# Where three engines' code lies: a second fetch block entered at the start, and 44 sums as a loop

## The chip, the core and the metric

The kernel runs on one core of a Trainium2 chip. A core has engines that each run their own instruction stream: TensorE (PE, matrix products), VectorE (DVE), ScalarE (ACT), GpSimd (POOL) and SyncE (SP, which here issues the loads). 16 DMA engines move data between device memory and the core. The metric is the device time of one execution in microseconds, lower is better.

## What is computed

One decoding step of a transformer block, batch 2, one new token, width 448, 16 heads of 256, a cache of 8192 keys and values for each head and batch entry, all in float32:

```python
q = (layernorm(x) @ wq)                                   # per head, per batch entry
scores = einsum("bhqd,bhkd->bhqk", q, k_cache) * Dh**-0.5
p = softmax(scores)
h = x + (einsum("bhqk,bhkd->bhqd", p, v_cache)) @ wo
n = layernorm(h)
out = h + ((n @ w_gate) * (n @ w_up)) @ w_down
```

Keys and values are 16 x 2 x 8192 x 256 floats each, 8 MB for every pair of head and batch entry, 537 MB in all. Each is used once.

## The kernel before

There are 32 pairs of head and batch entry (`NQ`). For each, 8192 keys lie as 128 partitions x 64 rows x 256. VectorE multiplies them with the query, which stands on every partition (`keys_times`, L358), and sums over the 256 (`summed`, L363); it takes the highest score (`highest`, L366). TensorE turns that column (`top`), VectorE negates its maximum (`negated`, L369), TensorE spreads it (`bias`), ScalarE takes the exponentials (`softmax`, L375), and TensorE multiplies them with the values (`mix`, L336: 32 products of two rows each). `turned` (L345) and L559 bring the result through `wo`, and `query` (L272, L277) makes the next head's query.

Pairs 1 to 30 run in hardware loops (`nc.Fori`), one for each of VectorE, ScalarE and TensorE, of 15 rounds with two pairs each; they meet through semaphores that are counted up by one engine and taken by another (`tell_of`, `take`, L319). SyncE's loads are written out in order: keys of a pair, values of the pair before, every eight pairs a piece of the weights. Keys have room for nearly two pairs, values for one, so each load waits until the last user of its room is done.

Ahead of the loops x is loaded (L185, by ScalarE's queue), turned by four transposes on TensorE (L241), and normalised in short steps between VectorE and TensorE (L244 to L266); then TensorE makes the queries of four heads (L272 to L302). [...] Its loop has 221 instructions, its whole program 1266, VectorE's 113, ScalarE's 161.

Behind the loops comes the last pair, then the two layers of the second half. For the last pair VectorE multiplies the keys in four parts of 16 rows; ScalarE sums rows 0 to 43 (`BY_ACT = 44`), one activation with accumulation and one read of the accumulator for each, written out (L526 to L529), VectorE sums the other 20. SyncE waits for both (L573) before it issues the second and third part of the last values (`LAST = (32, 24, 8)` rows) and the gate weights (L581), then the up weights (L583), then w_down in four pieces (`DOWN = (7, 4, 2, 1)` tiles, L587). TensorE follows: the last `mix`, the output projection, the gate and up products (L719) and the products with w_down (L778), which wait for each piece. VectorE copies the result (L785) and SyncE stores it.

Of the kernel before, what the change touches and what calls it, by code (L numbers as in the profile page):

```python
# [4 lines left out]
AF = mybir.ActivationFunctionType  # L5
ALU = mybir.AluOpType
AX = mybir.AxisListType
PE, DVE, ACT = (getattr(mybir.EngineType, n) for n in ("PE", "DVE", "Activation"))

B, D, H, SK, DH, F = 2, 448, 16, 8192, 256, 1792  # L10
EPS = 1e-5
P = 128
HALF = 64
DC = 4
# [3 lines left out]
HC = 16  # L18
# [9 lines left out]
BY_ACT = 44  # L28
# [45 lines left out]
def decode_block(nc, x, k_cache, v_cache, w, wg, wu, wd, out):  # L74
# [4 lines left out]


    names = ("x", "w", "k0", "k1", "k0a", "v", "g", "p", "d", "a", "zero", "dp", "ap", "pd", "pa", "da")
    names += ("dd", "aa", "gp", "first", "mixed", "heads")
    S = {n: Sem(nc, n) for n in names}
    late = [Sem(nc, f"late{i}") for i in range(len(LAST) + 1 + 2 + len(DOWN))]
    done = Sem(nc, "out")
    pe, dve, act, sp, pool = (
        Engine(e) for e in (nc.tensor, nc.vector, nc.scalar, nc.sync, nc.gpsimd)
    )

    def p_(instr):  # L90
        return S["p"].by(instr)

    def v_(instr):
        return S["d"].by(instr)

    def a_(instr):
        return S["a"].by(instr)
# [4 lines left out]
    def place(name, shape, offset=None):  # L102
        size = 4
        for n in shape[1:]:
            size *= n
        if offset is None:
            offset = at[0]
            at[0] += -(-size // 32) * 32
        return nc.alloc_sbuf_tensor_at(name, list(shape), F32, offset=offset).ap()
# [9 lines left out]
    ident = place("ident", (P, P))  # L119
# [3 lines left out]
    s_t = [place(f"s{i}", (P, NJ)) for i in range(2)]  # L123
# [15 lines left out]
    x_sb = place("x_sb", (B, DC * P))  # L139
# [30 lines left out]
    xT_ps = banks[6][:, : DC * B].rearrange("p (c b) -> p c b", b=B)  # L170
# [9 lines left out]
    def k_at(i, lo=0, hi=NJ):  # L180
        first = i % 2 * (NJ - OVER)
        return kb[:, first + lo : first + hi, :]


    x_in = S["x"].by(nc.scalar.dma_start(x_sb[:, :D], x.rearrange("b s d -> (b s) d")), 16)  # L185
    w_in = {0: S["w"].by(nc.sync.dma_start(wb[:, WQ:], w[0][:, WQ:]), 16)}

    def load_k(i, lo=0, hi=NJ, sem=None):
# [6 lines left out]
    t = S["g"].by(nc.gpsimd.memset(ident, 0.0))  # L195
    pool.wait(t)
    g_id = S["g"].by(
        nc.gpsimd.affine_select(
            out=ident, in_=ident, compare_op=ALU.not_equal, fill=1.0, base=0,
            pattern=[[-1, P]], channel_multiplier=1,  # L200
        )
    )
# [6 lines left out]
    def over_chunks(got, t):  # L209
        tok = v_(  # L210
            nc.vector.tensor_reduce(
                got, t[:, : DC - 1].rearrange("p c b -> p b c"), axis=AX.X, op=ALU.add
            )
        )
        dve.wait(tok)
        return v_(
            nc.vector.scalar_tensor_tensor(
                got, t[:, DC - 1, :], 0.5, got, op0=ALU.mult, op1=ALU.add
            )
        )  # L220
# [15 lines left out]
    )  # L236
    dve.wait(x_in)
    t = v_(nc.vector.tensor_copy(x_sb[:, D:], x_sb[:, D - HALF : D]))
    pe.wait(g_id, x_in, t)
    for c in range(DC):  # L240
        got = nc.tensor.transpose(xT_ps[:, c, :], x_sb[:, c * P : (c + 1) * P], ident[:B, :B])  # L241
    t = p_(got)
    dve.wait(t)
    t = v_(nc.vector.tensor_copy(xT, xT_ps))  # L244
    dve.wait(t)
    t = over_chunks(sum_x, xT)
    pe.wait(v_ones, t)
    t = p_(nc.tensor.matmul(mean_ps, ones, sum_x, start=True, stop=True))
    dve.wait(t)
    t = v_(  # L250
        nc.vector.scalar_tensor_tensor(
            xc, mean_ps[:, None, :].to_broadcast([P, DC, B]), -1.0 / D, xT,
            op0=ALU.mult, op1=ALU.add,
        )
    )
    dve.wait(t, g_xb)
    x_spread = spread(xb, xc, P)
    t = v_(nc.vector.tensor_mul(sq, xc, xc))
    dve.wait(t)
    t = over_chunks(sum_sq, sq)  # L260
    pe.wait(t)
    t = p_(nc.tensor.matmul(var_ps, ones, sum_sq, start=True, stop=True))
    act.wait(t, v_eps)
    t = a_(nc.scalar.activation(std, var_ps, AF.Sqrt, bias=eps_t, scale=1.0 / D))
    dve.wait(t)
    t = v_(nc.vector.reciprocal(rstd, std))  # L266
# [51 lines left out]
    def take(e, sem, n=1):  # L318
        e.wait_ge(S[sem].h, n).then_inc(S[sem].h, -n)  # L319

    def tell_of(instr, sem):
        instr.then_inc(S[sem].h, 1)
# [30 lines left out]
    last_act = []  # L353
    last = NQ - 1
    queries = qb.rearrange("p h b d -> p (h b d)")

    def keys_times(kt, q, to=None):
        return nc.vector.tensor_mul(  # L358
            kt if to is None else to, kt, q[:, None, :].to_broadcast([P, kt.shape[1], DH])
        )  # L360

    def summed(i, lo, hi, kt):
        return nc.vector.tensor_reduce(s_t[i % 2][:, lo:hi], kt, axis=AX.X, op=ALU.add)  # L363
# [4 lines left out]
    def negated():  # L368
        return nc.vector.tensor_reduce(nm, mT_ps, axis=AX.X, op=ALU.max, negate=True)  # L369
# [46 lines left out]
    first = v_(summed(0, NJ - HC, NJ, vb[:, :HC, :]))  # L416
    take(nc.vector, "k0", 16)
    t = v_(keys_times(k_at(0, 0, NJ - HC), qb[:, 0, 0]))
    dve.wait(t)
    t = v_(summed(0, 0, NJ - HC, k_at(0, 0, NJ - HC)))  # L420
# [4 lines left out]
    with nc.Fori(0, H - 1, engines=[DVE]) as g:  # L425
        for n in (1, 2):
            b = n % B
            off = nc.vector.snap((g + n // 2) % HEADS * (B * DH))
            q = queries[:, bass.ds(off + b * DH, DH)]
            parts = ((0, HC), (HC, NJ)) if b else ((NJ - HC, NJ), (0, NJ - HC))  # L430
            kt = k_at(n, *parts[0])
# [8 lines left out]
            kt = k_at(n, *parts[1])  # L440
# [7 lines left out]
    t = v_(  # L448
        nc.vector.tensor_reduce(
            sel16, ident.rearrange("p (g b r) -> p b r g", b=B, r=R)[:, :, 0, :],  # L450
            axis=AX.X, op=ALU.add,
        )
    )
# [5 lines left out]
    t = v_(  # L459
        nc.vector.tensor_scalar(  # L460
            share, sel16[:, None, :].to_broadcast([P, DC + 1, B]), -1.0 / D, None, op0=ALU.mult
        )
    )
# [12 lines left out]
    q = qb[:, (H - 1) % HEADS, B - 1]  # L476
    take(nc.vector, "k1", 16)
    dve.wait(behind(last - 1, 0))
    told["nm", last - 1] = v_(negated())
    ready = [v_(keys_times(k_at(last, 0, HC), q))]  # L480
    dve.wait(behind(last - 1, 2))
    d_rl[last - 1] = v_(nc.vector.reciprocal(rl_t[0], l_ps))
    for lo in range(HC, NJ, HC):
        ready.append(v_(keys_times(k_at(last, lo, lo + HC), q)))
    dve.wait(ready[-1])
    summed_last = v_(summed(last, BY_ACT, NJ, k_at(last, BY_ACT, NJ)))


# [1 line left out]
    with nc.Fori(0, H - 1, engines=[ACT]) as g:  # L490
        for b in range(B):
# [9 lines left out]
            got = turned_out(b, 0)  # L501
        tell_of(got, "ap")
        off = nc.scalar.snap(g % HEADS * (B * DH))
        for b in range(B):
            take(nc.scalar, "pa")
            got = nc.scalar.activation(  # L506
                queries[:, bass.ds(off + b * DH, DH)], q_ps[b], AF.Copy, scale=rstd[:, b : b + 1]
            )
# [14 lines left out]
        told["oT", i] = a_(turned_out(k, k))  # L523

    ends(last - 1)
    for k in range(BY_ACT):  # L526
        act.wait(ready[k // HC])
        kt = k_at(last)[:, k, :]
        t = a_(nc.scalar.activation(kt, kt, AF.Copy, accum_out=s_t[1][:, k : k + 1]))  # L529
    last_act.append(t)  # L530
    summed_at[last] = summed_last
    dve.wait(last_act[0], summed_last)
    told["m", last] = v_(highest(last))
# [6 lines left out]
        nc.gpsimd.sem_inc(S["gp"].h, HEADS)  # L540


    with nc.Fori(0, H - 1, engines=[PE], head_slot={PE: 0}) as g:
        with nc.Fori(0, B, engines=[PE]):
            take(nc.tensor, "dp")
            tell_of(top(), "pd")
            take(nc.tensor, "dp")
            tell_of(bias(), "pa")
            take(nc.tensor, "ap")
            tell_of(whole(), "pd")  # L550
            take(nc.tensor, "v", 16)
            tell_of(mix(0, NJ, vb), "pa")
            take(nc.tensor, "ap")
            tell_of(turned(), "pa")
        take(nc.tensor, "ap")
        take(nc.tensor, "gp")
        off = nc.tensor.snap(g % HEADS * WH)
        for c in range(2):
            nc.tensor.matmul(  # L559
                acc_ps, oT.rearrange("p c b r -> p c (b r)")[:, c], wb[:, bass.ds(off + c * D, D)],  # L560
                start=False, stop=False,
            )
        for b in range(B):
            tell_of(query(off, b), "pa")
# [4 lines left out]
    v_parts, lo = [], 0  # L569
    for n in LAST:  # L570
# [3 lines left out]
        to = kb[:, lo : lo + n, :]  # L574
# [9 lines left out]
    wd_in, lo = {}, 0  # L584
# [61 lines left out]
    lo, hi, v, there = v_parts[-1]  # L646
# [24 lines left out]
    def group(w, q):  # L671
# [8 lines left out]
        start=True, stop=False,  # L680
    )
    dve.wait(t_hq)
    t = v_(nc.vector.tensor_mul(mean_h, share, total[:, None, :].to_broadcast([P, DC + 1, B])))  # L683
    pe.wait(t)
    t = p_(
        nc.tensor.matmul(
            xc_ps.rearrange("p c b -> p (c b)"), ones, mean_h.rearrange("p c b -> p (c b)"),
            start=False, stop=True,
        )
    )  # L690
# [9 lines left out]
    t = v_(nc.vector.tensor_copy(xc_h, xc_ps[:, :DC]))  # L700
    dve.wait(t)
    t = v_(nc.vector.tensor_mul(sq_h, xc_h, xc_h))
    dve.wait(t)
    t = over_chunks(sum_h, sq_h)
# [36 lines left out]
    t = v_(nc.vector.tensor_scalar_add(ve, varh_ps, EPS))  # L741
# [30 lines left out]
    for k in range(NF):  # L772
        n, g = FF[k]
# [3 lines left out]
        for q in range(YN):  # L777
            got = nc.tensor.matmul(  # L778
                y_ps[32 * q : 32 * q + 32, :],
                hmT[n // 2][:, n % 2, g].rearrange("p b r -> p (b r)"),  # L780
                wd_t[:, k, q * YW : (q + 1) * YW], start=False, stop=(k == NF - 1),
            )
    t = p_(got)
    dve.wait(t)
    t = v_(nc.vector.tensor_copy(y, y_ps))  # L785
# [10 lines left out]
    t = done.by(nc.sync.dma_start(rows, eight(y)), 16)  # L796
# [60 lines left out]
```

## Time and profile before

| | |
|---|---|
| median of 3 runs (lowest to highest) | 1303.93 us (1303.85 to 1303.99) |
| the profiled execution | 1303.78 us |
| its span, first to last instruction | 1302.5 us |
| busy share of the span | DVE 86%, PE 38%, ACT 7% |
| DMA | 561.31 MB, 431 GB/s read over the span |
| instruction packets | queue q8: 5, 0.08 MB; queue q14: 3, 0.02 MB |

The profile is of one execution. Times in its rows are microseconds from the start of the span; "L336" is a line of the kernel. A row of the DMA part gives packets, bytes, and the time that they took as a share of 16 engines over the stretch. "hardware_dynamic" is data, "instruction" is code. In a row of stretches a packet counts with its whole length where it starts, so a short stretch can show a share above 1.

### The profile page before, as it was taken

Reading aid. Unit: us, or ns where it says so; the run is one execution under the profiler, and the core shown is the slowest. Engines: PE = TensorE matmul, PEld = TensorE weight load, DVE = VectorE, ACT = ScalarE, POOL = GpSimd, SP = SyncE. Lnnn points to the kernel's source line nnn. Section 1 sums busy time; section 2 is a strip of 40 time slices with the busy share of each in tenths; the row PEclk is TensorE's granted clock in tenths of the full one; section 3 lists DMA queues with packets and bytes.
Section 4 is the critical chain, followed back from the end, with each engine's and each line's share of the span. In section 5 each row is a group of like instructions: output and inputs, shape, how many; then the busy total and the mean of one; then the engine's idle time right before and its main releaser. Section 6 shows DMA issues by size and latency. Waiting matters only on the chain. (4 is left out here: it accounts for less than half of the span.)

```text
span 1302.5 us, 7994 instructions
## 1 busy us (share of the span) xinstructions
PE 494.4 (38%) x3182; PEld 200.4 (15%) x3182; DVE 1121.5 (86%) x272; ACT 86.9 (7%) x293; POOL 1.3 (0%) x8
## 2 busy tenths in 40 slices
PE   5034314343331433415343043432334333253548
PEld 5011102111110111202121021210112001020213
DVE  5998888889988699888899868998888897888970
ACT  2000000000000000000000000000000000000060
POOL 0000000000000000000000000000000000000000
PEclk9566657676666765667676576765667666676668
DMA  9999999999999999999999999999999999999998
GB/s 409 447 425 433 427 443 421 449 421 449 421 449 435 419 441 429 429 441 421 449 421 449 435 421 449 419 443 427 433 437 423 431 451 427 431 439 423 447 416 368
DMA packets 11412, 561.31 MB, mean 431 GB/s; under 512 B 1290, under 2 KB 1420, under 8 KB 1676
## 3 DMA queue, kind: packets, MB, share of 16 engines
q1 hardware_dynamic: 11400, 561.20, 99.7%
q8 instruction: 5, 0.08, 0.0%
q14 instruction: 3, 0.02, 0.0%
q10 hardware_dynamic: 4, 0.00, 0.0%
HBM read 561.19 MB, written 0.01 MB: 431 GB/s over the span
## 5 line engine op out<-in xcount | busy, mean ns | idle before, releaser
L358 DVE TENSOR_TENSOR kb<-kb,qb 128x12288 f32<-128x12288 f32 (+1 forms) x65 | 551.4, 8486 | 125.8 <-DVEq L319 125.7
L363 DVE TENSOR_REDUCE s<-kb 128x48 f32<-128x12288 f32 (+2 forms) x62 | 539.6, 8704 | 4.4
L336 PE MATMUL bank<-vb,p 128*2 128x512 f32 x1984 | 284.2, 734 | 408.5 <-PEq L319 408.5
L336 PEld LDWEIGHTS bank<-vb,p 128*2 128x2 f32 x1984 | 53.2, 96 | 610.6 <-issue 610.5
L328 PE MATMUL bank<-nm,ones 1*128 1x1 f32 x64 | 17.1, 334 | 202.8 <-PEq L319 202.4
L498 ACT ACTIVATE o_sb<-bank 128x512 f32<-128x512 f32 x30 | 17.9, 597 | 693.8 <-ACTq L319 693.8
L272 PE MATMUL bank<-wb,xb 128*128 (+1 forms) x228 | 60.7, 405 | 0.8 <-DMA wb<-in_w_dram 0.8
L325 PE MATMUL bank<-ident,m 128*1 128x128 f32 x32 | 10.3, 322 | 111.3 <-PEq L319 111.3
L328 PEld LDWEIGHTS bank<-nm,ones 1*128 1x128 f32 x64 | 15.3, 294 | 212.2 <-issue 210.8
L272 PEld LDWEIGHTS bank<-wb,xb 128*128 128x128 f32 x228 | 42.6, 201 | 19.9 <-issue 14.4
L345 PE MATMUL bank<-sel,o_sb 128*128 128x1 f32 x256 | 32.8, 249 | 29.9 <-PEq L319 29.1
L345 PEld LDWEIGHTS bank<-sel,o_sb 128*128 128x128 f32 x256 | 31.0, 191 | 58.8 <-issue 57.1
L559 PE MATMUL bank<-wb,oT 128*32 x60 | 32.6, 677 | 14.4 <-PEq L319 14.4
L331 PE MATMUL bank<-lsum,ones 128*128 128x1 f32 x64 | 17.4, 342 | 30.6 <-PEq L319 29.9
L372 ACT ACTIVATE nb<-bank 128x1 f32<-128x1 f32 x32 | 5.5, 171 | 330.0 <-ACTq L319 325.1
L277 PEld LDWEIGHTS bank<-wb,xb 128*128 128x128 f32 x152 | 23.7, 197 | 2.2
L277 PE MATMUL bank<-wb,xb 128*128 (+1 forms) x152 | 23.7, 279 | 0.0
L331 PEld LDWEIGHTS bank<-lsum,ones 128*128 128x128 f32 x64 | 15.6, 302 | 33.3 <-issue 32.4
L506 ACT ACTIVATE qb<-bank,rstd 128x256 f32 x30 | 14.2, 474 | 92.6 <-ACTq L319 92.6
L325 PEld LDWEIGHTS bank<-ident,m 128*1 128x1 f32 x32 | 2.6, 82 | 114.5 <-issue 114.5
L529 ACT ACTIVATE kb<-kb 128x256 f32<-128x256 f32 x44 | 17.6, 405 | 3.4 <-DVE kb L358 3.4
L683 DVE TENSOR_TENSOR mean_h<-share,total 128x10 f32<-128x10 f32 x1 | 0.2, 170 | 14.8 <-ACT hq L675 14.8
(100 smaller groups left out, 135.1 us busy)
## 6 DMA issues: line engine op xcount, KB each, us to landing
wb<-in_w_dram SPq DMA_DIRECT2D x3, 3584.0 KB, 37.5
kb<-in_A_k_cache_dram SPq DMA_DIRECT2D x1, 6144.0 KB, 25.3
kb<-in_A_v_cache_dram SPq DMA_DIRECT2D x1, 4096.0 KB, 31.9
wb<-in_w_dram SPq DMA_DIRECT2D x2, 1792.0 KB, 20.1
kb<-in_B_w_gate_dram SPq DMA_DIRECT2D x1, 3136.0 KB, 20.8
kb<-in_A_v_cache_dram SPq DMA_DIRECT2D x1, 3072.0 KB, 11.8
kb<-in_A_k_cache_dram SPq DMA_DIRECT2D x1, 2048.0 KB, 11.2
vb<-in_B_w_up_dram SPq DMA_DIRECT2D x1, 1792.0 KB, 20.0
```

The lines of the kernel that those rows point to most:

```text
L272: nc.tensor.matmul(q_ps[b], xb[:, c, b, :], wb[:, bass.ds(off + WQ + c * DH, DH)], start=(c == 0), stop=False,)
L277: got = nc.tensor.matmul(q_ps[b][:, k * P : (k + 1) * P], xb[:, DC - 1 + k, b, :], wb[:, bass.ds(off + WQ + (DC - 1) * DH, P)], start=Fals ...
L328: return nc.tensor.matmul(nb_ps, ones[:1, :], nm, start=True, stop=True)
L331: return nc.tensor.matmul(l_ps, ones, lsum, start=True, stop=True)
L336: got = nc.tensor.matmul(o_ps[own][g : g + 2, :], p_t[own][:, 2 * t : 2 * t + 2], v[:, j : j + 2, :], start=(t < 4), stop=(t >= NJ // 2 - 4),)
L345: got = nc.tensor.matmul(oT_ps[:, c : c + 1], o_sb[:, (2 * k + c) * P : (2 * k + c + 1) * P], sel[:, k : k + 1], start=(k == 0), stop=(k = ...
L358: return nc.vector.tensor_mul(kt if to is None else to, kt, q[:, None, :].to_broadcast([P, kt.shape[1], DH]))
L363: return nc.vector.tensor_reduce(s_t[i % 2][:, lo:hi], kt, axis=AX.X, op=ALU.add)
L498: tell_of(nc.scalar.activation(o_sb, o_ps[0], AF.Copy), "ap")
L506: got = nc.scalar.activation(queries[:, bass.ds(off + b * DH, DH)], q_ps[b], AF.Copy, scale=rstd[:, b : b + 1])
L529: t = a_(nc.scalar.activation(kt, kt, AF.Copy, accum_out=s_t[1][:, k : k + 1]))
L559: nc.tensor.matmul(acc_ps, oT.rearrange("p c b r -> p c (b r)")[:, c], wb[:, bass.ds(off + c * D, D)], start=False, stop=False,)
```

## The change

VectorE's stream, and ScalarE's behind its load of x, are aligned to slot 128 of a block of 256, with a branch over the padding. TensorE branches at its start to a new label "block1" at slot 0 of a block, waits there for x, runs the four transposes, and branches back to "start" (the condition, 0 < 1, always holds). Its loop lies behind the transposes in the same block, at slot 20. VectorE waits for the transposes on a semaphore of their own, "xt".

ScalarE's 44 sums become a loop of 11 rounds with four sums each; the addresses of the keys and of the sum come from registers. VectorE tells it by "ka", which counts groups of four rows, and the loop counts "summed" up for each round.

```diff
+    nc.vector.addr_align(256, offset=128, max_nops=0)
+    nc.scalar.addr_align(256, offset=128, max_nops=0)
+    def goto(label, here=None):
+        nc.br(label, engines=[PE])
+        if here is not None:
+            nc.switch_bb(here, parent=None)
+    goto("block1", "start")
...
-    pe.wait(g_id, x_in, t)
-    for c in range(DC):
-        got = nc.tensor.transpose(xT_ps[:, c, :], x_sb[:, c * P : (c + 1) * P], ident[:B, :B])
-    t = p_(got)
-    dve.wait(t)
+    x_there = (g_id, x_in, t)
+    dve.wait((S["xt"], 1))
...
-    ready = [v_(keys_times(k_at(last, 0, HC), q))]
+    keys_times(k_at(last, 0, HC), q).then_inc(S["ka"].h, HC // 4)
...
+        got = keys_times(k_at(last, lo, lo + HC), q)
+        if lo < BY_ACT:
+            got.then_inc(S["ka"].h, min(HC, BY_ACT - lo) // 4)
...
-    for k in range(BY_ACT):
-        act.wait(ready[k // HC])
-        kt = k_at(last)[:, k, :]
-        t = a_(nc.scalar.activation(kt, kt, AF.Copy, accum_out=s_t[1][:, k : k + 1]))
-    last_act.append(t)
+    with nc.Fori(0, BY_ACT // 4, engines=[ACT]) as g:
+        take(nc.scalar, "ka")
+        to = nc.scalar.snap(g * 4)
+        off = nc.scalar.snap(g * (4 * DH))
+        for k in range(4):
+            kt = flat_k[:, bass.ds(off + k * DH, DH)]
+            got = nc.scalar.activation(kt, kt, AF.Copy, accum_out=s_t[1][:, bass.ds(to + k, 1)])
+        tell_of(got, "summed")
+    last_act.append((S["summed"], BY_ACT // 4))
...
-    with nc.Fori(0, H - 1, engines=[PE], head_slot={PE: 0}) as g:
+    nc.tensor.addr_align(256, max_nops=0)
+    goto("queries", "block1")
+    for sem, n in x_there:
+        nc.tensor.wait_ge(sem.h, n)
+    for c in range(DC):
+        got = nc.tensor.transpose(xT_ps[:, c, :], x_sb[:, c * P : (c + 1) * P], ident[:B, :B])
+    tell_of(got, "xt")
+    turn = nc.alloc_registers("turn", engines=[PE])
+    nc.regs_mov(turn, 0)
+    nc.br_lt(turn, 1, on_true="start", on_false="queries", engines=[PE])
+    nc.switch_bb("queries", parent=None)
+    with nc.Fori(0, H - 1, engines=[PE], head_slot={PE: 20}) as g:
```

## Rows read from the trace of the kernel before

**Rows 1.** From the page: busy share of DMA by slices, bytes read, one load's time.
```profile
DMA  9999999999999999999999999999999999999998
...
HBM read 561.19 MB, written 0.01 MB: 431 GB/s over the span
...
kb<-in_A_v_cache_dram SPq DMA_DIRECT2D x1, 4096.0 KB, 31.9
```

**Rows 2.** The chain of waits from 1290: start us, us, what.
```profile
1271.19 28.21 DMA vb<-in_wd_dram
...
1299.44 0.99 PE bank L778 x24
...
1300.46 0.28 DVE y L785
```

**Rows 3.** Stretches: length, busy of five engines, granted clock, DMA share, GB/s.
```profile
1298.00:1298.25 0.25, 0.00 (x0) 0.00 (x0) 0.00 (x0) 0.00 (x0) 0.00 (x0) 1.00 0.52 197
1298.25:1298.50 0.25, 0.13 (x6) 0.13 (x9) 0.00 (x0) 0.00 (x0) 0.00 (x0) 1.00 0.40 154
1298.50:1298.75 0.25, 0.25 (x16) 0.25 (x16) 0.00 (x0) 0.00 (x0) 0.00 (x0) 1.00 0.37 143
1298.75:1299.00 0.25, 0.25 (x24) 0.25 (x16) 0.00 (x0) 0.00 (x0) 0.00 (x0) 1.00 0.31 117
1299.00:1299.25 0.25, 0.25 (x16) 0.10 (x5) 0.00 (x0) 0.00 (x0) 0.00 (x0) 1.00 0.25 95
1299.25:1299.50 0.25, 0.15 (x8) 0.06 (x8) 0.00 (x0) 0.00 (x0) 0.00 (x0) 1.00 0.10 36
```

**Rows 4.** DMA queues in 28 to 31: packets, MB, share of 16 engines.
```profile
q8 instruction: 1, 0.02, 2.1%
```

**Rows 5.** Timeline of the start: start us, us, engine, line, what, [idle before].
```profile
0.74 0.39 SPq L186 DMA_DIRECT2D wb<-in_w_dram  x1
...
2.45 0.55 PE L241 MATMUL bank<-ident,x_sb 2*128 2x2 f32 x4 [2.45 <-DVE x_sb L238]
...
24.28 0.93 PE L302 MATMUL bank<-x_sb,rows 2*32 2x448 f32 x2
...
27.08 12.96 DVE L358 TENSOR_TENSOR kb<-kb,qb 128x12288 f32<-128x12288 f32 x1 [5.22 <-DVEq L319]
```

**Rows 6.** Instruction packets in 1240:1245, then 1260:1296 (two), then 1299.5:1301.
```profile
q14 instruction: 2, 0.02, 0.8%
...
q8 instruction: 3, 0.05, 0.5%
q14 instruction: 1, 0.01, 0.1%
...
q8 instruction: 1, 0.02, 4.2%
```

**Rows 7.** The first stretch, columns as in rows 3.
```profile
0.00:1.50 1.50, 0.00 (x0) 0.00 (x0) 0.23 (x3) 0.13 (x1) 0.74 (x7) 1.00 0.00 0
```

**Rows 8.** Timeline of the last pair's sums and of the loads behind them.
```profile
1235.66 0.33 SPq L381 DMA_DIRECT2D kb<-in_A_v_cache_dram  x1
...
1244.57 0.42 ACT L529 ACTIVATE kb<-kb 128x256 f32<-128x256 f32 x1 [3.38 <-DVE kb L358]
...
1257.64 5.49 DVE L363 TENSOR_REDUCE s<-kb 128x20 f32<-128x5120 f32 x1
...
1262.07 0.19 ACT L529 ACTIVATION_READ_ACCUMULATOR kb<-kb 128x1 f32 x1
...
1263.15 0.81 SPq L381 DMA_DIRECT2D kb<-in_A_v_cache_dram  x2
```

**Rows 9.** Timeline of VectorE over the end of its loop body and the next round.
```profile
88.68 0.22 DVE L366 TENSOR_REDUCE m<-s 128x1 f32<-128x64 f32 x1
...
88.99 4.43 DVE L358 TENSOR_TENSOR kb<-kb,qb 128x4096 f32<-128x4096 f32 x1
```

More of the change, by code (lines that the diff above doesn't have):

```diff
@@ L81, in decode_block @@
     names = ("x", "w", "k0", "k1", "k0a", "v", "g", "p", "d", "a", "zero", "dp", "ap", "pd", "pa", "da")
-    names += ("dd", "aa", "gp", "first", "mixed", "heads")
+    names += ("dd", "aa", "gp", "first", "mixed", "heads", "ka", "summed", "xt")
     S = {n: Sem(nc, n) for n in names}
@@ L483, in decode_block @@
     for lo in range(HC, NJ, HC):
-        ready.append(v_(keys_times(k_at(last, lo, lo + HC), q)))
-    dve.wait(ready[-1])
+        got = keys_times(k_at(last, lo, lo + HC), q)
+        if lo < BY_ACT:
+            got.then_inc(S["ka"].h, min(HC, BY_ACT - lo) // 4)
+    dve.wait(v_(got))
     summed_last = v_(summed(last, BY_ACT, NJ, k_at(last, BY_ACT, NJ)))
@@ L525, in decode_block @@
     ends(last - 1)
-    for k in range(BY_ACT):
-        act.wait(ready[k // HC])
-        kt = k_at(last)[:, k, :]
-        t = a_(nc.scalar.activation(kt, kt, AF.Copy, accum_out=s_t[1][:, k : k + 1]))
-    last_act.append(t)
+    flat_k = k_at(last).rearrange("p j d -> p (j d)")
+    with nc.Fori(0, BY_ACT // 4, engines=[ACT]) as g:
[7 more added lines that the diff above has]
+    last_act.append((S["summed"], BY_ACT // 4))
     summed_at[last] = summed_last
```

## The prediction

> **What bounds the kernel now.** I read the page's first lines, then the chain of waits, then the last microseconds in quarter-microsecond stretches, and only then the instruction queues. The page says it in two lines: the DMA row is at nine tenths or more in 39 of 40 slices, and 561.19 MB are read at 431 GB/s [rows 1]. The chain of waits ends with the last load of w_down, issued at 1271.19 and landed at 1299.40; behind it come 0.99 us of matmuls, a 0.28 us copy and the store of the output [rows 2]. So the time is: bytes over the DMA rate, plus about 3 us of tail. Nothing on an engine counts unless it delays a load or the tail.
>
> The end of the loads is ragged [rows 3]. From 1298.00 the DMA share falls as 0.52, 0.40, 0.37, 0.31, 0.25, 0.10 in six stretches of 0.25 us. Their sum is 1.95, times 0.25 is 0.49 us of all 16 engines, spread over 1.5 us. Had the 16 DMA engines ended together, the last byte would have come 1.5 - 0.49 = 1.0 us earlier. I read this as some engines running late, since a share of 0.25 is 4 engines of 16.
>
> What makes an engine late is, by my reading, code. A 16 KB instruction packet stands in 28 to 31 us, just after TensorE ended its last matmul ahead of the loop at 24.28 + 0.93 = 25.21 [rows 4, 5]; it takes 2.1% of 3 us x 16 engines = 1.01 us of one engine. Two 8 KB packets (0.8% of 5 x 16 = 0.64, so 0.32 us each) come at 1240 to 1245, three of 16 KB and one of 8 KB at 1260 to 1296, one more of 16 KB after 1299.5, behind the data [rows 6]. [...] Ahead of the end this makes four packets of 16 KB and three of 8 KB, and four engines still work at 1299.0 to 1299.25: one for each large fetch, if each falls on another engine.
>
> **The change, part by part.**
>
> *Where fetches go.* [...] TensorE's 1266 do not shrink: its other three large fetches stay, and the single small one of 1260 to 1296, which comes while SyncE issues its last loads, stays too. Removed from the busy stretch: 1.01 + 2 x 0.32 = 1.65 us of single engines.
>
> *What that is worth.* Pooled over 16 engines it would be 1.65 / 16 = 0.10 us. But each engine has its own share of every load, so the end is that of the latest engine. Of four engines late by a large fetch one is freed and three stay; the stretch 1299.25 to 1299.50 holds 0.10 x 0.25 x 16 = 0.4 engine-us for the last ones, so the next latest ends about 0.1 us before the last. Both ways the gain is 0.1 us. The bounds: 0 if the freed engine is not the last; 1.0 if the rest of the unevenness went too; and a loss of 1.0 where a fetch falls a second time on an engine that is already late. I take -0.10.
>
> *TensorE's way through the start.* The four transposes move into block 1 with two or three waits, a register move and a branch each way. Cost at nothing: they run at 2.45 for 0.55 us and wait for VectorE's copy as before, and VectorE sits idle 5.22 us until the product of 27.08 can start [rows 5]; a start up to 5 us later is lost in that wait.
>
> *The tail of TensorE.* The loop now starts at slot 20 of its block, so everything behind it meets each block boundary 20 slots earlier. The fetch after 1299.5 came with the matmuls of the last three w_down tiles; each tile is 16 slots (4 column groups, two passes, a weight load and a matmul each), so it moves back 1.25 tiles into the group before, ahead of the landing of 1299.40 [rows 2]. That puts its packet near 1299.0 to 1299.4, where 4 to 2 engines still carry data. On an idle one it costs nothing, on a busy one up to 1.0 us.
>
> *ScalarE's loop.* Now 44 sums at one per 0.40 us run from 1244.57 to 1262.26, VectorE's share of the sums until 1257.64 + 5.49 = 1263.13, and SyncE's next load is issued when both are there: cover 0.87 us [rows 8]. In the loop each 4 sums (1.6 us, 17.69 us over 44 times 4) have one semaphore taken, some 8 register steps, an addition and a branch. The nearest row is VectorE's loop edge, 88.68 to 88.99: 0.31 us from start to start with a semaphore, a branch and a register step in it, most of it beside the 0.22 us of the instruction before [rows 9]. Lower end: all of it beside the sums, nothing but a first start some 0.2 us later, inside the cover. Upper end: nothing beside them, one 0.31 for the edge and one for each sum, 5 x 0.31 x 11 = 17 us. I take the lower, because the row shows the edge of a loop hidden behind even a short instruction, and 1.6 us is five times the edge.
>
> *Sum.* The profiled execution took 1303.78 us for a span of 1302.5, the median of three is 1303.93, 0.15 above. -0.10 with 0 and 0: 1303.7 for the profiled one, 1303.8 for the median.
>
> **The rivals.**
>
> 1. *ScalarE's loop sets the pace (slower).* Place: the wait of SyncE for the 44 sums. Behind it stand the second and third part of the last values, the gate weights, and all later loads. The price starts when the sums end more than 0.87 us later plus what the queue still holds at 1263.15: the first part of the values, issued at 1235.66 and 31.9 us under way, lands on the last engine at 1267.56, on the first about 1.0 us earlier, and a new load needs about 1.0 us from issue to the first byte (0.74 to after 1.5) [rows 1, 5, 7, 8], so 1267.56 - 1.0 - 1.0 - 1263.15 = 2.4. It decides from 3.3 us of delay, 0.30 us in each of the 11 rounds. At one 0.31 us edge exposed, 3.4 us: 0.1 us, no more than noise. At two, 6.8 us: 3.5 us, 1307.3. At the upper end 17 us: 13.7 us, 1317.5. For it: registers address both operands of every sum. Against it: the hidden edge [rows 9].
>
> [...]
>
> 3. *A fetch on a late engine at the end.* The last fetch, moved ahead of the last bytes, meets one of the 2 to 4 engines still at work: up to 1.0 us, 1304.3 to 1304.8. For it: the 20 slots. Against it: so far each large fetch seems to have had an engine to itself, and then it meets one that has ended.
>
> 4. *More is freed.* If the packets at the start go onto an engine that is late anyway, or the small ones were what the last engine carried, up to half of the 1.0 us goes: 1303.3.
>
> **How the numbers follow.** The forecast, 1303.5 to 1304.1, gets 0.62; rival 1 with a cost 0.08 (0.04 of it beyond 2.6 us); rival 2 with a miss 0.11, most of it within 0.2 us of before; rival 3 0.10; rival 4 0.09. Two in ten may lie outside: the range goes from 1303.1 (rival 4) to 1304.9 (rivals 2 and 3). What a measurement tells from no change is 0.2%, 2.6 us; every case but the far part of rival 1 and an unseen gain stays inside. Faster 0.02, same 0.94, slower 0.04.
>
> **What would show it.** Right: in the profile after, 16 KB and 8 KB instruction packets within the first 3 us and none in 28 to 31 or 1240 to 1245 of the 8 KB kind; three large ones and one small between 1235 and 1299; the last DMA quarter still ragged, with three to four engines at the end; the 44 sums at 0.40 us each, ending by 1263. Wrong: a large packet in 28 to 31 us or TensorE idle for more than a microsecond behind the transposes (rival 2); sums at 0.45 us or more and a dip of the DMA share at 1265 (rival 1); the last landing after 1299.9 beside an instruction packet (rival 3). The step I trust least is that the other three late engines hold the end where it is.

## The result: 1305.8 us, 1.8 us more, and the profile after

| | before | changed |
|---|---|---|
| median of 22 runs (lowest to highest) | 1304.0 us (1303.76 to 1305.09) | 1305.8 us (1304.35 to 1306.65) |
| ratio, 95% interval | | 1.0013 [1.0007, 1.0018] |
| the profiled execution, its span | 1303.78, 1302.5 us | 1304.55, 1303.2 us |

The change costs 1.8 us: by the bound of 0.2% no change, but not nothing, and above the predicted range. The profiled execution is one of the quicker ones and shows 0.8 of the 1.8 us. A second profiled execution of the changed kernel (after_look) took 1306.46 us and is used beside it.

The page's first lines stand where they stood [rows 1]:

```profile
span 1303.2 us, 8103 instructions
...
DMA  9999999999999999999999999999999999999998
...
HBM read 561.19 MB, written 0.01 MB: 431 GB/s over the span
```

The instruction queues of the changed kernel in the stretches 0 to 3.5, 3.5 to 8, 1235 to 1299 and 1299.5 to 1302 (packets, MB, share of 16 engines), against [rows 4, 6]:

```profile
q8 instruction: 1, 0.02, 3.3%
...
q14 instruction: 2, 0.02, 0.9%
...
q8 instruction: 3, 0.05, 0.3%
q14 instruction: 1, 0.01, 0.0%
...
q8 instruction: 1, 0.02, 2.4%
```

The fetches went where the prediction put them: one of 16 KB and two of 8 KB at the start, none in 28 to 31 us, three large and one small ahead of the end. But none lay in the idle time: by the trace the large one began at 1.96 us and the small ones at 3.61 and 5.70, with the first loads under way since 1.75. And the large one took 3.3% x 3.5 x 16 = 1.85 us of an engine, where that of 28 to 31 had taken 1.01. (This differs between executions: 1.42 in the one of 1306.46 us, 1.79 and 1.12 in pe_alone and after_w_first below.)

Timeline of the changed kernel's start, TensorE, VectorE, then SyncE (start us, us, engine, line, what, [idle before]); it answers to [rows 5]:

```profile
2.45 0.55 PE L564 MATMUL bank<-ident,x_sb 2*128 2x2 f32 x4 [2.45 <-DVE x_sb L250]
3.74 0.56 PE L257 MATMUL bank<-sum_x,ones 128*128 128x2 f32 x2 [0.74 <-DVE sum_x L229]
...
9.04 1.22 PE L281 MATMUL bank<-wb,xb 128*128 128x256 f32 x2 [2.19 <-DMA wb<-in_w_dram]
...
13.92 4.43 DVE L367 TENSOR_TENSOR vb<-kb,qb 128x4096 f32<-128x4096 f32 x1 [6.57 <-DMA kb<-in_A_k_cache_dram]
...
28.57 12.96 DVE L367 TENSOR_TENSOR kb<-kb,qb 128x12288 f32<-128x12288 f32 x1 [5.22 <-DVEq L328]
...
64.02 0.33 SPq L202 DMA_DIRECT2D kb<-in_A_k_cache_dram  x1
```

The same places in the kernel before:

```profile
3.65 0.58 PE L248 MATMUL bank<-sum_x,ones 128*128 128x2 f32 x2 [0.65 <-DVE sum_x L217]
...
7.58 2.93 PE L272 MATMUL bank<-wb,xb 128*128 128x256 f32 x6 [0.79 <-DMA wb<-in_w_dram]
...
12.43 4.43 DVE L358 TENSOR_TENSOR vb<-kb,qb 128x4096 f32<-128x4096 f32 x1 [5.15 <-DMA kb<-in_A_k_cache_dram]
...
62.53 0.33 SPq L190 DMA_DIRECT2D kb<-in_A_k_cache_dram  x1
```

Read down the two columns of starts. The transposes are at 2.45 in both, the next matmul 0.09 later. Then TensorE waits for the first weights, 2.19 us where it was 0.79, and its queries start 1.46 later; VectorE's products start 1.49 later (13.92 for 12.43, 28.57 for 27.08), and SyncE issues the third load of keys 1.49 later. Look at the idle time ahead of the second product: 5.22 us, as before. The wait in which the lateness was to be lost came along with it, because what ends it, the landing of the first keys, came late too (28.44 for 26.95). The first product also starts 0.03 us behind a landing of keys in both kernels, when its query has been ready for half a microsecond: VectorE waits for the late keys, not for the late query. The rows of the 48 rows of keys and of the first weights (KB, us from issue to landing), changed kernel, then before:

```profile
kb<-in_A_k_cache_dram SPq DMA_DIRECT2D x1, 6144.0 KB, 26.8
...
wb<-in_w_dram SPq DMA_DIRECT2D x1, 1792.0 KB, 8.3
```

```profile
kb<-in_A_k_cache_dram SPq DMA_DIRECT2D x1, 6144.0 KB, 25.3
...
wb<-in_w_dram SPq DMA_DIRECT2D x1, 1792.0 KB, 6.8
```

The trace has 16 landings for each of these loads, which I read as one part for each DMA engine, and the user starts behind the last. Of the first weights they lie between 7.00 and 7.53 us before; in the changed kernel 14 lie between 7.09 and 7.77, one at 8.12 and the last at 9.00, and TensorE starts at 9.04. The packet of code, 1.85 us of one engine, so held up the whole load: its last part came 1.47 us later.

Where the queue then runs out, stretches of 0.5 us in the execution of 1306.46 us (columns as [rows 3]: DMA share and GB/s last), and two of them of the kernel before:

```profile
64.50:65.00 0.50, 0.00 (x0) 0.00 (x0) 0.50 (x1) 0.00 (x0) 0.00 (x0) 0.50 1.08 393
65.00:65.50 0.50, 0.00 (x0) 0.00 (x0) 0.50 (x1) 0.00 (x0) 0.00 (x0) 0.50 0.62 262
65.50:66.00 0.50, 0.00 (x0) 0.00 (x0) 0.50 (x1) 0.00 (x0) 0.00 (x0) 0.50 1.37 524
66.00:66.50 0.50, 0.00 (x0) 0.00 (x0) 0.50 (x1) 0.00 (x0) 0.00 (x0) 0.50 1.05 393
66.50:67.00 0.50, 0.19 (x4) 0.14 (x8) 0.50 (x1) 0.00 (x0) 0.00 (x0) 0.50 1.50 524
```

```profile
64.50:65.00 0.50, 0.00 (x0) 0.00 (x0) 0.50 (x1) 0.00 (x0) 0.00 (x0) 0.50 3.82 1573
65.00:65.50 0.50, 0.00 (x0) 0.00 (x0) 0.50 (x1) 0.00 (x0) 0.00 (x0) 0.50 0.95 393
```

A packet counts where it starts. Before, the engines take up the third load nearly together, most of them in one half microsecond; in the changed kernel they start over some 2 us. In between, the records leave each engine without a packet for 0.72 us on average (0.42 in the quicker execution, 0 before). The packets that follow also take longer. In the last row of the changed kernel 524 GB/s are four packets of 64 KB, and 1.50 x 0.5 x 16 = 12 us of engines are 3.0 us for each; in the row of 64.50 before, 1573 GB/s are twelve, at 2.55 us each; in the middle of the stream such a packet takes 2.42.

At the end, the last piece of w_down, whose 16 parts landed over 1.59 us before, lands over 2.67 in the slower execution. In the quicker one it is 1.77, no more than in a kernel that loses nothing (2.01 in loop_alone below); there all parts are later, by 0.70 us on average. The chain of the changed kernel's quicker execution, against [rows 2], and its end, against [rows 3]:

```profile
1271.96 28.19 DMA vb<-in_wd_dram
...
1300.19 1.00 PE bank L805 x24
...
1301.21 0.27 DVE y L812
```

```profile
1299.25:1299.50 0.25, 0.25 (x16) 0.25 (x14) 0.00 (x0) 0.00 (x0) 0.00 (x0) 1.00 0.36 143
1299.50:1299.75 0.25, 0.25 (x21) 0.25 (x16) 0.00 (x0) 0.00 (x0) 0.00 (x0) 1.00 0.29 108
1299.75:1300.00 0.25, 0.25 (x16) 0.09 (x4) 0.00 (x0) 0.00 (x0) 0.00 (x0) 1.00 0.28 108
```

The DMA of the chain is the last piece but one, and the 24 matmuls are those of the last two pieces. They start at 1300.19 for 1299.44, 0.75 us later; the last piece lands at 1300.70 for 1299.95, 0.75 later too, which is what the profiled execution is longer. The share of 0.28 is 4.5 engines of 16; 0.75 us earlier the kernel before had 0.25 [rows 3]. The landings say it more plainly: in both kernels five of the 16 parts of the last piece land more than a microsecond behind the first. Not one engine fewer is late.

### The profile page after: what moved, and what is told of

Same layout as the page of the kernel before. It is cut to its first block, busy times and chain, and to the rows that moved or that the text cites. A ratio compares the mean times of both kernels' runs of the same rounds, so it can differ in the third digit from the quotient of the medians.

```text
span 1303.2 us, 8103 instructions
## 1 busy us (share of the span) xinstructions
PE 496.9 (38%) x3182; PEld 200.5 (15%) x3182; DVE 1121.2 (86%) x272; ACT 86.9 (7%) x293; POOL 1.3 (0%) x8
## 2 busy tenths in 40 slices
DMA packets 11412, 561.31 MB, mean 431 GB/s; under 512 B 1290, under 2 KB 1420, under 8 KB 1676
## 5 line engine op out<-in xcount | busy, mean ns | idle before, releaser
L586 PE MATMUL bank<-wb,oT 128*32 x60 | 35.4, 729 | 14.5 <-PEq L328 14.5
L544 ACT ACTIVATE kb<-kb x44 | 17.6, 399 | 3.6 <-ACTq L328 3.6
L378 DVE TENSOR_REDUCE nm<-bank 1x1 f32<-1x128 f32 x32 | 8.7, 272 | 5.4 <-PE bank L334 3.0
```

What stands on the lines that cost most here:

```text
L544: got = nc.scalar.activation(kt, kt, AF.Copy, accum_out=s_t[1][:, bass.ds(to + k, 1)])
L586: nc.tensor.matmul(acc_ps, oT.rearrange("p c b r -> p c (b r)")[:, c], wb[:, bass.ds(off + c * D, D)], start=False, stop=False,)
```

## The experiments

Two theories. *The start*: the fetch among the first loads makes a chain late (first weights and keys, products, release of the keys' room, third load of keys), and past some cover the DMA engines run dry. *The code itself*: fetches collide on late engines, or the new loop or branches cost something. (The expectations call the first theory A; rival B is the two 8 KB packets, rival C the loop of sums or the slot of TensorE's tail.) Each new kernel of the table ran 11 times, beside 27 to 33 runs of the kernel before (medians 1303.96, 1303.96, 1304.02 in the three groups). "Late" is the issue of the third load of keys against 62.53; "dry" the mean time without a packet near 65 us; "spread" from the first to the last landing of the last piece, all three from the profiled execution. That execution is the quickest of its kernel, or within 0.2 us of it, for most rows; for late15 and late15_w_first it is among the slowest.

| kernel | median us (range) | ratio [95%] | late | dry | spread |
|---|---|---|---|---|---|
| changed | 1305.80 (1304.35 to 1306.65) | 1.0013 [1.0007, 1.0018] | 1.49 | 0.42 | 1.77 |
| pe_alone | 1305.68 (1304.93 to 1306.45) | 1.0013 [1.0004, 1.0022] | 1.46 | 0.51 | 2.03 |
| no_pe | 1304.89 (1303.93 to 1306.68) | 1.0008 [0.9999, 1.0017] | 0.31 | 0 | 2.02 |
| loop_alone | 1304.04 (1303.72 to 1305.73) | 1.0000 [0.9991, 1.0009] | 0.01 | 0 | 2.01 |
| late07 | 1305.97 (1304.06 to 1306.62) | 1.0015 [1.0006, 1.0024] | 0.70 | 0 | 1.90 |
| late15 | 1305.76 (1305.09 to 1306.57) | 1.0013 [1.0004, 1.0022] | 1.59 | 0.52 | 3.49 |
| late30 | 1306.32 (1306.09 to 1306.79) | 1.0019 [1.0010, 1.0028] | 3.06 | 1.69 | 1.54 |
| after_w_first | 1303.96 (1303.58 to 1305.93) | 1.0000 [0.9991, 1.0009] | 1.03 | 0 | 1.72 |
| late15_w_first | 1303.83 (1303.69 to 1306.01) | 0.9998 [0.9989, 1.0007] | 1.89 | 0 | 3.56 |
| before_w_first | 1304.05 (1303.72 to 1304.66) | 1.0001 [0.9992, 1.0010] | 0.41 | 0 | 1.67 |
| no_pe_w_first | 1304.09 (1303.79 to 1304.23) | 0.9999 [0.9990, 1.0008] | 0.57 | 0 | 1.84 |
| after_wait | 1306.27 (1306.02 to 1309.20) | 1.0017 [1.0008, 1.0026] | 2.48 | 0 | 1.77 |

**Which part of the change.** pe_alone is the kernel before with TensorE's way to block 1 and back and slot 20 of its loop, nothing else. no_pe is the changed kernel with these taken out:

```diff
-    goto("block1", "start")
...
-    x_there = (g_id, x_in, t)
-    dve.wait((S["xt"], 1))
+    pe.wait(g_id, x_in, t)
+    for c in range(DC):
+        got = nc.tensor.transpose(xT_ps[:, c, :], x_sb[:, c * P : (c + 1) * P], ident[:B, :B])
+    t = p_(got)
+    dve.wait(t)
...
-    with nc.Fori(0, H - 1, engines=[PE], head_slot={PE: 20}) as g:
+    with nc.Fori(0, H - 1, engines=[PE], head_slot={PE: 0}) as g:
```

> The kernel before with TensorE's part alone: transposes in the second block, loop at slot 20; nothing of VectorE and ScalarE. Theory A: a large packet near 2 us, the last of the first weights at 8.5 us or later, third load of keys at 63.5 or later, DMA share under 0.9 at 64 to 66, time 1305.0 to 1306.5 and a spread of over 1 us. Rival B (8 KB packets): 1304. Rival C, loop of sums: 1304; tail's slot: 1305 to 1306 but with no idle near 65 us.

> The changed kernel without TensorE's part: transposes back in the first block, loop at slot 0; VectorE's and ScalarE's code still begins in the second block and the 44 sums are a loop. Theory A (TensorE's 16 KB packet among the first loads delays the first weights by 1.5 us on one DMA engine, and with them the queries, VectorE and the issue of the third load of keys, so that all DMA engines run dry near 65 us): the large packet is back near 28 us, the first weights land by 8.2 us, the third load of keys is issued by 63.2, no idle at 64 to 66, time 1303.6 to 1304.2 with the narrow spread of before. Rival B (the two 8 KB packets at the start do it): 1305 to 1306.5 as with the whole change. Rival C (the loop of sums or the layout of the tail costs it): the sums' loop is still here, so 1305 or more if it is the loop, 1304 if it is the slot of TensorE's tail.

First pe_alone, then no_pe: TensorE's wait for the first weights and SyncE's third load.

```profile
9.01 1.22 PE L276 MATMUL bank<-wb,xb 128*128 128x256 f32 x2 [2.16 <-DMA wb<-in_w_dram]
...
63.99 0.33 SPq L197 DMA_DIRECT2D kb<-in_A_k_cache_dram  x1
```

```profile
7.89 2.50 PE L277 MATMUL bank<-wb,xb 128*128 128x256 f32 x5 [0.82 <-DMA wb<-in_w_dram]
...
62.84 0.33 SPq L195 DMA_DIRECT2D kb<-in_A_k_cache_dram  x1
```

TensorE's part alone gives 1.7 of the 1.8 us and nearly the whole lateness. Without it 0.31 us of lateness is left, the length of one 8 KB packet (the first weights land at 7.84 for 7.53), and 0.9 us of time, more than I expected, whose interval reaches to nothing.

**Lateness without moved code.** late07 and late15 are the kernel before with a memory fill on VectorE ahead of the second product; late30 has two of the larger fill.

```diff
     take(nc.vector, "k0", 16)
+    v_(nc.vector.memset(wb[:, :1376], 0.0))   # late07: :688
```

> The kernel before with one more VectorE instruction, a fill of 128 x 1376 floats in room of the weights that is not yet used, ahead of the product of the first 48 rows of keys: no code moves, VectorE is late by about 1.45 us. Theory A: the third load of keys is issued near 64.0 instead of 62.53, DMA share under 0.9 at 64 to 66, time 0.4 to 0.8 us above before, 1304.4 to 1304.8. Rivals B and C, where a late start is hidden in the queue: 1304.0.

> The kernel before with a fill of half the size, 128 x 688 floats, ahead of the product of the first 48 rows: VectorE is late by about 0.6 us and the third load of keys is issued near 63.1 to 63.6. Theory A with a cover of about 1.1 us in the queue (the last of the first values ends at 65.1, a load needs 1.0 us and was issued at 62.53): nothing runs dry, 1303.9 to 1304.2. Rival A2 (there is no cover; each us that VectorE is late costs more than a us): 1304.6 to 1305.0.

> The kernel before with two fills of 128 x 1376 floats: VectorE is late by about 2.4 us, the third load of keys is issued near 65.2. Theory A: all DMA engines are idle for about 1.4 to 1.8 us near 65 to 67; with what the one fill cost beyond its idle time, 1306.5 to 1307.5. Rival A2 (the cost of a late VectorE is a fixed step, from engines that end unevenly after any stop): 1305.5 to 1306.5 as with one fill.

late15, VectorE and SyncE:

```profile
27.61 1.21 DVE L419 MEMSET wb<- 128x1376 f32 x1 [5.53 <-DVEq L319]
28.74 12.89 DVE L358 TENSOR_TENSOR kb<-kb,qb 128x12288 f32<-128x12288 f32 x1
...
64.12 0.33 SPq L190 DMA_DIRECT2D kb<-in_A_k_cache_dram  x1
```

No instruction has moved between blocks, and the time is that of the changed kernel: 1305.76. But the loss is not lateness less a cover, as I expected, and all three came out otherwise: 0.63 us of fill costs 2.0 us, 1.21 us costs 1.8, two of them 2.36. Each of these is known to about 1.2 us, so they cannot be put in order; what is plain is that a fill of half the size costs no less.

The packet records account for much of it. Where something ran dry near 65 us, the first 64 KB packets of the third load took 2.8 to 3.1 us on average, for 2.42 in the stream. So each engine lost its idle time and some 0.3 to 0.6 us more. Against before, the parts of that load land later on average by 0.80 us (changed), 0.91 (pe_alone), 1.02 (late15), 1.23 (the execution of 1306.46) and 2.23 (late30); in late07, with nothing dry, by 0.05. The rest is unevenness, since the time is that of the last part: in late15 the last piece of w_down lands 1.06 us later on average and 2.62 later in its last part. In late30 all engines had run dry and took up the load together: its last piece is 2.34 us later in its first part (1300.70 for 1298.36), and its spread is 1.54. The profiled execution of late07, the quickest of its 11 (1304.06), shows no dry time, so the cause of its median is argued, not shown.

**Cover given back.** The second piece of the weights (3584 KB, 8.5 us at 431 GB/s) is issued ahead of the third load of keys, not behind it:

```diff
+            sp.wait(q_first)
+            load_w(1)
...
-            if off == 0 and k < H // HEADS:
-                sp.wait((S["heads"], k * HEADS) if k else q_first)
+            if off == 0 and 0 < k < H // HEADS:
+                sp.wait((S["heads"], k * HEADS))
```

It goes into the changed kernel, the kernel before, the changed one without TensorE's part, and the kernel before with 1.4 us of fills (late15_w_first, three on a bank of PSUM, the `bank` that the matmuls of the rows above write).

> The whole change, and the second piece of the weights (3.5 MB, 8.5 us of the queue) is issued behind the first values instead of behind the third load of keys. The first weights land late as in the changed kernel, but the queue holds 8.5 us more when VectorE is late. Theory A: no idle near 65 us, time back to 1303.5 to 1304.3 with a narrow spread, though VectorE's first product still starts near 14 us. Rivals B and C without the queue running dry (a late engine or a slower tail): 1305 to 1306.5 as before.

> The kernel before with the second piece of the weights issued behind the first values; no code moves. Theory A: in the kernel before nothing runs dry in most runs, so 1303.8 to 1304.0, same; against the changed kernel with the same order of loads (1303.96) it shows what the moved fetches are worth alone: 0.0 to 0.2 us. If moved fetches help by the 0.1 us of the prediction, this is that much slower than the changed one.

> The kernel before with three fills of a PSUM bank (about 1.6 us) in the place of the one fill, and the second piece of the weights issued behind the first values. No code moves. Theory A: VectorE is later than with one fill, but the queue holds 8.5 us more, so nothing is idle near 65 us: 1303.7 to 1304.2, narrow. Rival (VectorE's delay itself is carried to the end, by the sums or the tail): 1305.5 or more.

> VectorE's and ScalarE's code in the second block and the loop of sums, TensorE as before, and the second piece of the weights issued behind the first values. Theory A (the two 8 KB packets among the first loads make VectorE some 0.3 us late, and without the profiler that is enough to let the queue run dry): with the longer queue the 0.9 us of the same kernel without it are gone, 1303.7 to 1304.1. Rival (the loop of sums or ScalarE's place costs them): 1304.5 to 1305.0 stays.

SyncE in after_w_first and in late15_w_first:

```profile
63.56 0.33 SPq L202 DMA_DIRECT2D kb<-in_A_k_cache_dram  x1
```

```profile
64.42 0.33 SPq L190 DMA_DIRECT2D kb<-in_A_k_cache_dram  x1
```

The load is still issued 1.0 and 1.9 us late, and nothing is lost: 1303.96 and 1303.83. The reorder gains nothing by itself (1304.05), so what it takes away is the loss: the loss hangs on what the queue holds when the third load is issued. The single runs stand apart as the medians do. Ten of 11 are at or below 1304.27 in after_w_first and 1303.99 in late15_w_first; none is below 1304.93 in pe_alone or late15. (The profiled execution of late15_w_first, 1306.01, was the one of its 11 above 1304; one engine landed 3.56 us behind the first there, with nothing dry near 65 us. A single late engine so has other causes too, which stay open.)

**The rest.** loop_alone is the kernel before with the loop of sums only, without alignment. after_wait is the changed kernel with SyncE's first load held until x is turned, so that the packets run ahead of all its loads:

```diff
+    sp.wait((S["xt"], 1))
     w_in = {0: S["w"].by(nc.sync.dma_start(...), 16)}
```

> The kernel before with the loop of 44 sums alone; no code is aligned and TensorE is as before. Theory A: sums at 0.40 us, the loads of the tail issued at the same time, 1303.8 to 1304.1. Rival (the loop costs): 1304.5 or more.

> The whole change, and SyncE's first load waits for the transposes, so that TensorE's 16 KB packet is done before the first data. All loads start some 2.3 us later, and nothing else is changed. Theory A (what harms is the packet among the first loads): the first weights land on all engines within 0.7 us, the third load of keys is issued at most 0.8 us late against the loads around it, and no DMA engine runs dry near 67 us; 1305.9 to 1306.6, the 2.3 us of the later start. Rival (the way over the blocks costs wherever the packet lies): 2.3 us on top of the change, 1307.5 to 1309.

> The changed kernel once more, for a second profile of it. Theory A: w's last landing, VectorE's first product and the issue of the third load of keys are 1 to 2 us later than before, idle near 65 us, and the time is the first landing of the last load plus the spread of its 16 landings plus 3.84 us, as in the other profiles; 1304.4 to 1306.6.

The loop costs nothing. In after_wait the first parts of the first weights land 2.26 us later (9.26 for 7.00), all 16 within 0.76 us, and the median is 2.25 us above before's: the price is the later start (SyncE's first load is issued 2.30 us later, its third load of keys 2.48). The spread stays within 0.76 us until 1259 us and is 1.77 at the end all the same. The late fetches can be counted in it: behind the 16 KB packet of 1262.9 one of the 16 parts lands over 1.6 us behind the first, behind that of 1277.3 two, behind that of 1295.8 three.

## Why the prediction was wrong

**The step that failed** is "TensorE's way through the start ... Cost at nothing", with its reason, "VectorE sits idle 5.22 us until the product of 27.08 can start; a start up to 5 us later is lost in that wait". I took the wait as room. It ends with a landing, and by my reading that landing waits for the same DMA engine that the fetch held up: 15 parts of the keys were there by 27.55, the last at 28.44 for 26.95, VectorE started 1.49 us later, and nothing of it was lost in the wait. Room after a load is no cover for what delays the load. I had also taken the start as time in which a fetch meets no data. The DMA share is 0.00 until 1.5 us [rows 7], but the first packet of code began at 1.96, behind the first packets of data at 1.75. I also never asked how much queue SyncE had in hand at its first dependent load. The profiles say less than 1.0 us: none dry at 0.70 us of lateness (late07), dry at 1.02 (the execution of 1306.46), both without the earlier weights. Beyond that, lateness alone does not set the dry time: 1.49 us left 0.42 dry, 1.02 left 0.72.

**Where the fetches go** was right, packet for packet, though not their hour: 2 to 6 us, not all within the first 3. Which engine's code a packet carries was my reading. The runs bear it out: with TensorE's part alone (pe_alone) the 16 KB packet stands in 0 to 3.5 us (3.2% of 16 engines) and none in 28 to 31; without that part (no_pe) it is back in 28 to 31 (2.1%), and the two of 8 KB stand at the start (0.6% of 0 to 3.5 us, 0.4% of 3.5 to 8). No run shows the 1.65 us of single engines that the prediction takes as removed: the packets of 28 to 31 and 1240 to 1245 us are gone from there, but all three lie among the first loads, with 1.85 us for the large one and 0.9% x 4.5 x 16 = 0.65 for the two small ones. **What that is worth**, -0.10 us, cannot be told from 0: with the loss at the start covered, 1303.96 stands against 1304.05 for the same order of loads without the change, and each ratio is known to 0.09%. after_wait shows why little was to be had: with the early packets out of the way the end is no less ragged, since three large fetches behind 1260 us make three engines late. That was the step I trusted least, and it held. One reading behind it was off: the landing of 1299.40 is that of the last piece but one, and the last landed at 1299.95. The 0.1 us between the two latest engines, taken from a share in which packets count where they start, is what the landings show (1299.85 and 1299.95), by luck.

**The rivals.** ScalarE's loop does not set the pace. Its sums in the changed kernel, with VectorE's share and SyncE's next load, against [rows 8]:

```profile
L544 ACT ACTIVATE kb<-kb x44: 398/399/417, 1243.9 to 1261.1; - x44
...
1256.70 5.49 DVE L372 TENSOR_REDUCE s<-kb 128x20 f32<-128x5120 f32 x1
...
1262.21 1.71 SPq L390 DMA_DIRECT2D kb<-in_A_v_cache_dram  x2
```

From 1243.9 to 1261.1 in 43 steps is 0.40 us each, as written out; VectorE's share ends at 1262.19 and sets the issue. TensorE's way back cost no second packet at the start, and its next matmul is 0.09 us later. The late fetch is still there (1300.09 us for 1299.80), but a kernel that has it too loses nothing (after_w_first). None of the rivals named a delay of the first loads; the case "slower by some 2 us" had no place in the range because the one step that held it was set to nothing without bounds.

What the way over the blocks cost TensorE itself was 0.09 us; the DMA engine that carried the packet spent 1.85 us on it here, among the first loads.

**Open**: why 0.6 us of lateness costs as much as 1.5; why the engines take up a late load unevenly; which engine a packet falls on; why the profiled executions of several kernels are among their quickest.

## What to carry to other kernels

Here a code fetch took a DMA engine for 1.85 us, and the load beside it was as late as its latest part: 9.00 us for 7.53. Moved into the first loads, the fetch delayed what hung on them, down to the third load of keys (1.49 us). In a kernel bound by DMA the place to look is the first load whose issue waits for computed work. Before an idle time is booked as cover, ask what ends it and whether the change delays that too. Lateness that exceeds the queue was met here with queue: a load whose own wait had ended long before, issued earlier, took the whole loss away (1303.96 us for 1305.80), though it gained nothing on the kernel before (1304.05).

## What the runs showed of the hardware

- A 16 KB instruction packet took 1.12 to 1.85 us among the first loads (four executions), 1.31 ahead of them (after_wait), 1.01 in the stream (28 to 31 us before).
- Behind such a packet one of the 16 parts of every later load was late, in the kernel before, with nothing dry near 65 us: from 48 to 1238 us one part lands some 1.8 us behind the first, the others within 0.6. In after_wait one, two and three are late behind the three late packets.
- The taken branch of TensorE back to its first block brought no fetch: 0.74 us of idle time ahead of the next matmul for 0.65, and no second 16 KB packet before 1262 us.
- The DMA engines that ran dry did not restart together: the third load's landings at 85 us in the execution of 1306.46 lay evenly over 2.0 us; before they lay within 0.4, but for one engine at 1.77. And the first 64 KB packets behind a dry stretch took 2.8 to 3.1 us on average, for 2.42 in the stream.
